# Weight and chunk stores issued from GpSimd's queue instead of SyncE's, in a fused Fourier-mixing and gated MLP kernel

## The chip, the cores and the metric

The kernel runs on one core of a Trainium2 chip. The metric is the device time of one execution in microseconds (us); the figure quoted for a kernel is the median of its runs. Engines are named as in the profile: PE is TensorE's matmuls and PEld its weight loads, DVE is VectorE, ACT is ScalarE, POOL is GpSimd and SP is SyncE. A DMA is issued by SP, ACT or POOL, each of which has a queue of its own; the bytes are moved by 16 DMA engines.

## The reference

`x` has 2048 rows of 512. It is normalised, passes through a Fourier mixing in one branch and an MLP in the other, and the two are multiplied and added to `x`:

```python
def _A_ref(x, dft_seq_re, dft_seq_im, dft_hid_re, dft_hid_im):
    a = jnp.einsum("bsd,ed->bse", x, dft_hid_re)
    b = jnp.einsum("bsd,ed->bse", x, dft_hid_im)
    return jnp.einsum("ts,bse->bte", dft_seq_re, a) - jnp.einsum("ts,bse->bte", dft_seq_im, b)

def _B_ref(x, w1, b1, w2, b2):
    h = jnp.einsum("bsd,df->bsf", x, w1) + b1
    r = jnp.where(h > 0, h, 0)
    return jnp.einsum("bsf,fd->bsd", r * r, w2) + b2

xn = _layernorm(x)
s = _A_ref(xn, A_dft_seq_re, A_dft_seq_im, A_dft_hid_re, A_dft_hid_im)
g = _silu(_B_ref(xn, B_w1, B_b1, B_w2, B_b2))
return x + s * g
```

The sequence matrices are 2048 x 2048, the hidden ones 512 x 512, `w1` is 512 x 1792 and `w2` 1792 x 512, all in float32.

## The kernel before, in words

Every float32 operand is split into a high part (ScalarE, `split_hi`, L134) and a low part (VectorE, `split_lo`, L137), and a product is made in three passes of matmuls. Most products are tiled two by two in Winograd's form: seven products instead of eight, with sums of the operands made by VectorE beforehand.

The kernel runs in this order. First the sequence matrices are multiplied with the normalised `x`, in 8 chunks of 256 rows (`c`), each in 8 steps (`j`). Chunks 0 and 1 are made in plain products (`products`, L368, matmuls at L377); chunks 2 to 7 in Winograd's form (the loop at L596, matmuls at L362). One step of chunks 2 to 7 takes 42 matmuls. Then come the products of the chunk results with the hidden matrices (`YUnit`), then those with `w1` (`HUnit`), then those with `w2` (from L1043), with the gate and the output.

A step's piece of the sequence matrix is 512 KB. SP loads it (`load_c`, L273) into one of three buffers tagged `u`. VectorE makes its sums in place (`step_sums`, L284 to L286), and ScalarE and VectorE split it into one of two buffers `ga` and `gb` (`step_split`, L320), from which TensorE reads. In step n the code makes the sums for step n + 2, splits for step n + 1, and issues the load for step n + 4. A load waits until the split has read the buffer's old contents.

Beside the steps, other work is made ahead. `EARLY` (L39) says at which step a piece of it is done:

- Weights: `weight` (L396) loads one weight's raw tiles on SP, makes its sums, splits them into a buffer `wd0` or `wd1`, and stores the result to device memory in two parts of 768 and 1024 KB (L412). This is done for the four hidden-matrix tiles (`d0` to `d3`, stored in `WDD`) and for three tiles of `w1` (`v0`, `v1`, `v6`, stored in `W1D`). They are read back much later: `WDD` by `load_wd` (L459, tiles named `wdp`), `W1D` by `load_w1` (L680).
- Chunk results: the eight results of a chunk are combined by VectorE during the next chunk's steps (`closing_of`, L335, operations at L343) into a buffer tagged `e`, 1024 KB. For chunks 2 to 6 it is stored to `PQD` when step 4 of the next chunk has made its last operation (L617). The results of chunks 0 and 1 (L562, L607) and of chunk 7 (L922) are stored elsewhere in the code. They are read back by `load_pq` (L419), from chunk 0's on.

The order on each engine is the order in which the code is written; there is no scheduler. A DMA-issuing engine takes its DMAs one after the other: a DMA that waits for its source or its buffer holds up those behind it on the same engine. SP issues all loads and, in this kernel, all stores but two kinds: the `w1` results and the mixing results, which ScalarE issues in its own queue (`hd<-h` and `y<-y`). POOL issues seven DMAs near the end, which add parts of `x` to the output tile in place (`add_x`, L899).

Of the kernel before, what the change touches and what calls it, by code (L numbers as in the profile page):

```python
# [8 lines left out]
F32 = mybir.dt.float32  # L9
# [119 lines left out]
def fnet_gated_kernel(ctx, tc, x, xt, ct, wd, w1, w2, b1, b2, out):  # L129
    nc = tc.nc  # L130
# [8 lines left out]
    def split(*parts):  # L139
        split_hi(*parts)  # L140
        split_lo(*parts)

    def copy(to, src, scale=1.0):
        nc.scalar.activation(to, src, AF.Copy, scale=scale)
# [12 lines left out]
    PQD = [dram.tile([P, 2, 4, 256], F32, name=f"pqd{c}") for c in range(NC)]  # L157
# [6 lines left out]
    def bank(tag, name):  # L164

        return acc.tile([P, 512], F32, tag=tag, name=name)

    def buf(tag, shape, name, dtype=F32):
        return pool.tile(shape, dtype, tag=tag, bufs=3 if tag == "u" else 1, name=name)
# [105 lines left out]
    def plain_parts(c, j, hs=slice(0, 2)):  # L275
        if (c, j) not in part:
            part[c, j] = operand_buf("g" + "ab"[j % 2], f"g{c}_{j}", 0 if (c, j) == (PLAIN - 1, NJ - 1) else 3 if j in TURNED else 1, (2, 4, CW))
        g, r = part[c, j], raw[c, j]
        s = slice(2 * hs.start, 2 * hs.stop)
        return g[:, HI, s], g[:, LO, s], r[:, s]  # L280
# [24 lines left out]
    def step_load(n):  # L305
        if n < len(steps):
            load_c(*steps[n])
        elif n - len(steps) + YFIRST < 6:
            y_load(n - len(steps) + YFIRST)

    def step_sums(n):
        if n < len(steps):
            u = raw[steps[n]]
            sums_b(u[:, 4:8], u)

    def step_split(n):
        if n < len(steps):
            s = steps[n]
            u = raw.pop(s)
            g = part[s] = buf("g" + "ab"[s[1] % 2], [P, 2, 7, CW], f"g{s[0]}_{s[1]}", F32R)  # L320
            split(g[:, HI], g[:, LO], u[:, 1:8])
# [13 lines left out]
    def closing_of(part_, ms, room):  # L335

        copy(part_(C21), halves(ms[1]))
        for k in room:
            copy(room[k], ms[k])
        for to, m, frm, op in ((C11, 2, C21, ALU.add), (C22, 6, C21, ALU.add), (C21, 7, C22, ALU.subtract),  # L340
                               (C12, 5, C22, ALU.subtract), (C22, 5, C21, ALU.add), (C12, 3, C12, ALU.add),
                               (C21, 4, C21, ALU.subtract)):
            nc.vector.tensor_tensor(part_(to), halves(room.get(m, ms[m])), part_(frm), op=op)  # L343
            yield
# [3 lines left out]
    def chunk_part(e):  # L348

        v = e.rearrange("p (h i m n) -> p h m i n", h=2, i=2, m=2)  # L350
        return lambda k: v[:, PART[k][0], PART[k][1]]

    def some(steps_, n):
        for _ in range(n):
            next(steps_)

    def mm(ps, w, mv, first, last):

        ps = ps.rearrange("p (i d t) -> p d i t", i=2, d=2)
        for d in range(2):  # L360
            for a_, b_ in PASSES:
                nc.tensor.matmul(ps[:, d], w[:, a_, d * P:(d + 1) * P], halves(mv(b_)),  # L362
                                 start=first and d == 0 and (a_, b_) == (HI, HI),
                                 stop=last and (a_, b_) == (LO, HI), skip_group_check=True)
# [21 lines left out]
    def go(*names):  # L386


        for v in names:
            if v[0] == "h" and int(v[1:]) >= NTC * NP:  # L390
                continue
            if v not in making:
                making[v] = makers[v[0]](int(v[1:]))
            next(making[v])

    def weight(n, raw_, sums_, to, k, e=None, turn=False):  # L396

        if e:
            e = buf(e, [P, 8, 256], f"{n}rt")
            r, t = e[:, 0:4], e[:, 4:8]  # L400
        else:
            r, t = buf("pq00", [P, 4, 256], f"{n}r"), buf("pq01", [P, 4, 256], f"{n}t")
        nc.sync.dma_start(r, raw_)
        yield
        if turn:
            copy(r[:, I22:I21 + 1], r[:, I22:I21 + 1], -1.0)
        sums_(t, r)
        yield
        g = buf(f"wd{int(k)}", [P, 2, 7, 256], f"{n}g", F32R)
        for q, src in ((slice(0, 3), r[:, 1:4]), (slice(3, 7), t)):  # L410
            split(g[:, HI, q], g[:, LO, q], src)
            nc.sync.dma_start(to[:, :, q], g[:, :, q].bitcast(F32))  # L412
            yield

    makers["d"] = lambda n: weight(f"wd{n}", wd[n], sums_b, WDD[n], n % 2, "e" if n == 1 else None, True)
    makers["v"] = lambda n: weight(f"w1{n}", w1[n], sums_w1, W1D[n], 0)

    def load_pq(n, x_):
# [84 lines left out]
    g = plain_parts(0, 1)  # L503
# [11 lines left out]
    for j in range(1, NJ):  # L515
# [19 lines left out]
        g = plain_parts(*order[j + 1])  # L535
# [51 lines left out]
    def last_out(k, op):  # L587
        to = last.rearrange("p (h i m d t) -> p h d m i t", h=2, i=2, m=2, d=2)[:, k // 2, k % 2]
        op(to, accs[1][k].rearrange("p (m i t) -> p m i t", m=2, i=2))
# [6 lines left out]
    for n, s in enumerate(steps):  # L596
        c, j = s
        if j == 0:
            ms = {k: bank(tag, f"m{k}_{c}") for k, tag in
                  {1: "bb", 2: "b20", 6: "b21", 3: "b30", 5: "b31", 7: "b32", 4: ("ba", "bc")[c % 2]}.items()}  # L600
        g = part.pop(s)
        for p in FIRST if j == 0 and c > PLAIN else ORDER:
            if p == 4 and n == 0:
                step_sums(2)
                step_split(1)
                last_out(3, copy)
                nc.sync.dma_start(PQD[1].rearrange("p h k n -> p (h k n)"), last)  # L607
            a, b = PRODUCTS[p]
            mm(ms[p], XC[j][:, a], lambda b_: g[:, b_, b], j == 0, j == NJ - 1)
        if n:  # L610
            step_sums(n + 2)
            step_split(n + 1)
        step_load(n + 4)
        if closing:
            some(closing, LATER.get(j, 0))
            if j == max(LATER):
                nc.sync.dma_start(PQD[c - 1].rearrange("p h k n -> p (h k n)"), e)  # L617
                closing = None
        if j == NJ - 1:
            e = buf("e", [P, 2048], f"c{c}")  # L620
            room = {}
            if c < NC - 1:
                room = buf("pq10", [P, 2, 512], f"left{c}")
                room = {7: room[:, 0], 5: room[:, 1], 3: buf("pq11", [P, 512], f"left3_{c}")}
            closing = closing_of(chunk_part(e), ms, room)
            some(closing, 2)
        if s == (PLAIN, 4):
            nc.vector.transpose(stats_t, stats.rearrange("p m h j -> p (m h j)"))
            for q in range(4):
                nc.sync.dma_start(rows[:, q * 32:(q + 1) * 32], stats_t[q * 32:(q + 1) * 32, :])  # L630
        go(*EARLY.get(s, ()))
# [326 lines left out]
    for u in range(2, NC):  # L958
        n = 2 * u + 2
# [83 lines left out]
    for n in range(NTC * NP):  # L1043
        c, p = divmod(n, NP)
# [37 lines left out]
        if p == NP - 1 and not last:  # L1082
            e = buf("e", [P, 4, 512], f"z{c}")
# [16 lines left out]
    e = buf("u", [P, 4, 512], f"z{c}")  # L1100
# [54 lines left out]
def _launch(arrays, out_shape):  # L1155
    import numpy as np
    import concourse.bacc as bacc
    from concourse.bass_utils import run_bass_kernel_spmd

    nc = bacc.Bacc("TRN2", target_bir_lowering=False, num_devices=1, dynamic_dma_scratch_size=1024)  # L1160
    feed, args = {}, []
    for name, v in arrays.items():
        v = np.ascontiguousarray(v)
        feed[f"in_{name}"] = v
        args.append(nc.dram_tensor(f"in_{name}", v.shape, mybir.dt.from_np(v.dtype), kind="ExternalInput").ap())
    args.append(nc.dram_tensor("out_0", out_shape, F32, kind="ExternalOutput").ap())
    with tile.TileContext(nc, schedule_with_timeline_sim=True) as tc:
        fnet_gated_kernel(tc, *args)
    r = run_bass_kernel_spmd(nc, [feed], core_ids=[0])
    return r.results[0]["out_0"]  # L1170
# [25 lines left out]
```

## Time and profile before

| | |
|---|---|
| time, median of 3 runs | 673.54 us (673.42 to 674.33) |
| time of the profiled execution | 673.52 us |
| its span, first to last instruction | 671.7 us |
| TensorE (PE) busy | 665.4 us, 99% of the span |
| VectorE (DVE) busy | 597.3 us, 89% |
| ScalarE (ACT) busy | 379.0 us, 56% |
| GpSimd (POOL) busy | 8.8 us, 1% |
| moved by DMA | 150.82 MB, mean 225 GB/s |

The profile is of one execution. Times are counted from the span's start. A row of a group or of a timeline gives the engine, the line of the code, the operation, what is written and read (`out<-in`), the count, and times in us; "idle before" is how long the engine had waited, and the arrow names what ended that wait. `SPq` stands for SP's queue of DMA-issuing instructions. "To landing" is the time from a DMA's issue to the completion that others can wait for.

### The profile page before, as it was taken

What the parts mean: (1) busy time and instruction counts of PE and PEld (TensorE: products, weight loads), DVE (VectorE), ACT (ScalarE), POOL (GpSimd) and SP (SyncE); (2) the same over time, 40 slices, a digit from 0 to 9 for tenths busy, and PEclk for the clock granted to TensorE, in tenths of its full rate; (3) what the DMA queues carried; (4) which work ended last, traced back from release to release, by engine and by line L of the source; (5) the groups of instructions that cost most, each with busy time, mean ns of one, the idle gap of its engine ahead of it and who ended that gap; (6) DMA issues with size and microseconds to landing.
All of it is one profiled execution on the core that took longest, in us unless ns stands there. A gap on an engine that the chain in (4) does not pass through costs nothing.

```text
span 671.7 us, 13186 instructions
## 1 busy us (share of the span) xinstructions
PE 665.4 (99%) x5438; PEld 646.5 (96%) x5438; DVE 597.3 (89%) x833; ACT 379.0 (56%) x524; POOL 8.8 (1%) x11
## 2 busy tenths in 40 slices
PE   8999999999999999999999999999999999999997
PEld 5888889999999999999999999999999999999997
DVE  7997888999999999799899989877887889999997
ACT  6856554534445454444365547788778765454451
POOL 0000000000000000000000000000000000101011
PEclk9999999999999999999999999999999999999999
DMA  8635768646556774759688557665755866777765
GB/s 306 212 100 218 255 232 277 214 148 213 211 168 225 248 286 162 261 164 344 200 296 279 194 188 297 222 246 209 267 183 198 326 241 212 181 230 176 232 205 156
DMA packets 51739, 150.82 MB, mean 225 GB/s; under 512 B 4960, under 2 KB 19552, under 8 KB 50272
## 3 DMA queue, kind: packets, MB, share of 16 engines
q1 hardware_dynamic: 43568, 129.28, 57.1%
q10 hardware_dynamic: 6208, 18.88, 7.1%
q0 software_dynamic: 1904, 1.84, 1.9%
q8 instruction: 42, 0.69, 0.4%
q14 instruction: 17, 0.14, 0.1%
HBM read 101.98 MB, written 47.99 MB: 223 GB/s over the span
## 4 chain that ended last, share of the span: by engine, by line
PE 94%; DVE 2%; DMA 2%; ACT 1%; issue 0%; SPq 0%; DVEq 0%; ACTq 0%
PE m L362 32%; PE m_o L861 15%; PE r_B L755 13%; PE r_A L755 9%; PE pq_b L377 8%; PE r_C L755 4%; PE r_D L755 4%; PE m_last L861 4%; PE pq_ba L377 2%; PE pq_bc L377 1%; PE pq_bb L377 1%; DMA u<-in_ct 1%; DMA x<-in_x 1%; DVE g L137 1%; DVE z L1111 0%; DVE z L911 0%
## 5 line engine op out<-in xcount | busy, mean ns | idle before, releaser
L362 PEld LDWEIGHTS m<-g,xc 128*128 128x128 f32 x2016 | 229.1, 188 | 0.3 <-DVE g L137 0.2
L362 PE MATMUL m<-g,xc 128*128 128x256 f32 x2016 | 229.3, 276 | 0.1
L134 ACT ACTIVATE g<-u 128x1792 fp32r<-128x1792 f32 (+2 forms) x65 | 99.0, 1523 | 132.1 <-PE m L362 92.6
L137 DVE TENSOR_TENSOR g<-u,g 128x1792 fp32r<-128x1792 f32 (+2 forms) x65 | 116.8, 1797 | 19.3 <-ACT g L134 18.8
L861 PE MATMUL m_o<-w,g 128*128 128x256 f32 x882 | 100.5, 276 | 0.0
L861 PEld LDWEIGHTS m_o<-w,g 128*128 128x128 f32 x882 | 100.3, 188 | 0.0
L134 ACT ACTIVATE g<-hr 128x1792 fp32r<-128x1792 f32 (+2 forms) x31 | 48.2, 1566 | 39.9 <-DVE hr L296 17.7
L755 PE MATMUL r_B<-xT,w 128*128 128x256 f32 x504 | 66.5, 276 | 0.0
L377 PE MATMUL pq_b<-g,xc 128*128 128x512 f32 x240 | 65.2, 391 | 1.0 <-ACT xc L134 1.0
L755 PEld LDWEIGHTS r_B<-xT,w 128*128 128x128 f32 x504 | 61.4, 188 | 0.0
L137 DVE TENSOR_TENSOR g<-hr,g 128x1792 fp32r<-128x1792 f32 (+2 forms) x31 | 56.7, 1838 | 3.0 <-ACT g L134 2.8
L377 PEld LDWEIGHTS pq_b<-g,xc 128*128 128x128 f32 x240 | 44.8, 188 | 11.3 <-ACT xc L134 1.9
L755 PE MATMUL r_A<-xT,w 128*128 128x256 f32 x336 | 42.8, 276 | 0.0
L755 PEld LDWEIGHTS r_A<-xT,w 128*128 128x128 f32 x336 | 40.2, 188 | 0.0
L755 PE MATMUL r_B<-wdp,yg 128*128 128x256 f32 x288 | 35.9, 277 | 0.0
L284 DVE TENSOR_TENSOR u<-u 128x512 f32<-128x512 f32 x48 | 32.9, 685 | 3.0 <-DMA u<-in_ct 3.0
L755 PEld LDWEIGHTS r_B<-wdp,yg 128*128 128x128 f32 x288 | 34.1, 188 | 0.1
L861 PE MATMUL m_last<-w,g 128*128 128x256 f32 x294 | 33.5, 276 | 0.0
L861 PEld LDWEIGHTS m_last<-w,g 128*128 128x128 f32 x294 | 33.4, 188 | 0.0
L137 DVE TENSOR_TENSOR yg<-yraw,yg 128x1792 fp32r<-128x1792 f32 x13 | 26.2, 2018 | 0.7 <-ACT yg L134 0.7
L134 ACT ACTIVATE yg<-yraw 128x1792 fp32r<-128x1792 f32 x13 | 22.2, 1707 | 5.4 <-DVE yraw L293 4.4
L755 PE MATMUL r_D<-xT,w 128*128 128x256 f32 x168 | 23.6, 276 | 0.0
(187 smaller groups left out, 876.8 us busy)
## 6 DMA issues: line engine op xcount, KB each, us to landing
u<-in_ct SPq DMA_DIRECT2D x63, 512.0 KB, 3.9
hd<-h ACTq DMA_DIRECT2D x28, 512.0 KB, 4.0
hr<-hd SPq DMA_DIRECT2D x28, 512.0 KB, 3.7
wdp<-wdd SPq DMA_DIRECT2D x8, 896.0 KB, 7.2
yraw<-pqd SPq DMA_DIRECT2D x13, 512.0 KB, 6.0
pqd<-c SPq DMA_DIRECT2D x6, 1024.0 KB, 6.2
w<-w1d SPq DMA_DIRECT2D x6, 896.0 KB, 8.2
y<-y ACTq DMA_DIRECT2D x8, 512.0 KB, 5.5
```

Source lines behind the costliest of these rows:

```text
L134: nc.scalar.activation(hi, src, AF.Copy)
L137: nc.vector.tensor_tensor(lo, src, hi.bitcast(F32), op=ALU.subtract)
L284: nc.vector.tensor_tensor(t[:, 0:2], r[:, 0:1].to_broadcast([P, 2, 256]), r[:, 1:3], op=ALU.add)
L362: nc.tensor.matmul(ps[:, d], w[:, a_, d * P:(d + 1) * P], halves(mv(b_)), start=first and d == 0 and (a_, b_) == (HI, HI), stop=last and ( ...
L377: nc.tensor.matmul(accs[c][k], w, part[c, j][:, b_, 2 * h:2 * h + 2], start=j == 0 and h == 0 and (a_, b_) == (HI, HI), stop=j == NJ - 1 a ...
L755: nc.tensor.matmul(self.region(REGION[k]), w, mv, start=i == 0 and k in (1, 7), stop=i == len(ops) - 1, skip_group_check=True)
L861: nc.tensor.matmul(m[:, i * 256:(i + 1) * 256], ready[n][:, a_, H_SLOT[a], i * P:(i + 1) * P], W2[p][:, b_, b], start=p == 0 and i == 0 an ...
```

## The change

The store of each part of a weight (L412) and the store of a chunk's result in the loop over the steps (L617) are issued by POOL in place of SP. The loads, the other stores and all arithmetic stay where they are.

```diff
@@ -409,7 +409,7 @@
         g = buf(f"wd{int(k)}", [P, 2, 7, 256], f"{n}g", F32R)
         for q, src in ((slice(0, 3), r[:, 1:4]), (slice(3, 7), t)):
             split(g[:, HI, q], g[:, LO, q], src)
-            nc.sync.dma_start(to[:, :, q], g[:, :, q].bitcast(F32))
+            nc.gpsimd.dma_start(to[:, :, q], g[:, :, q].bitcast(F32))
             yield
 
@@ -614,7 +614,7 @@
         if closing:
             some(closing, LATER.get(j, 0))
             if j == max(LATER):
-                nc.sync.dma_start(PQD[c - 1].rearrange("p h k n -> p (h k n)"), e)
+                nc.gpsimd.dma_start(PQD[c - 1].rearrange("p h k n -> p (h k n)"), e)
                 closing = None
```

On SP's queue, at step 4 of chunk 6, the change reads as follows (`-` is gone; `u7_0` and `u7_1` are pieces of the sequence matrix loaded ahead for chunk 7, `wdp0` a stored weight that is loaded back in two halves, `pqd5` the stored result of chunk 5):

```order
 L459 DMA wdp0_2852<-wdd0_83 128x1792
 L273 DMA u7_0_2902<-in_ct 128x1024
-L617 DMA pqd5_80<-c5_2626 128x2048
 L459 DMA wdp0_2852<-wdd0_83 128x1792
 L273 DMA u7_1_2955<-in_ct 128x1024
```

The store is gone from between the two loads, and the second half of `wdp0` follows `u7_0` directly.

On POOL's queue, the later stores and the first of the adds near the end (`w1d1` and `w1d6` are tiles of `w1`, `z0` the output tile; `+` is new):

```order
+L412 DMA w1d1_88<-w11g_2081 256x1x768
+L412 DMA w1d1_88<-w11g_2081 256x1x1024
+L617 DMA pqd4_79<-c4_2188 128x2048
+L412 DMA w1d6_89<-w16g_2519 256x1x768
+L412 DMA w1d6_89<-w16g_2519 256x1x1024
+L617 DMA pqd5_80<-c5_2626 128x2048
+L617 DMA pqd6_81<-c6_3057 128x2048
 L899 DMA z0_6599<-in_x 128x2x256 x2
```

POOL had nothing to issue before that first add; now 19 stores stand ahead of it.

## The prediction

> **What bounds the kernel now.** I read the busy time by stretches first, then what TensorE waited for, then the one place where the chain of waits leaves TensorE, and last the queues. Busy time by stretches (start:end, length, then busy us and instruction count of PE, PEld, DVE, ACT and POOL, granted clock, DMA share, GB/s):
>
> ```profile
> 0.00:20.00 20.00, 17.77 (x68) 12.52 (x69) 16.42 (x43) 13.96 (x31) 0.20 (x4) 1.00 0.80 289
> 20.00:635.00 615.00, 614.95 (x5085) 601.51 (x5084) 549.23 (x746) 351.77 (x479) 5.00 (x4) 1.00 0.66 225
> 635.00:671.70 36.70, 32.70 (x289) 32.50 (x287) 31.64 (x46) 13.27 (x16) 3.65 (x3) 0.98 0.64 185
> ...
> 95.00:270.00 175.00, 175.00 (x1546) 174.95 (x1545) 161.63 (x203) 81.84 (x66) 0.00 (x0) 1.00 0.63 217
> 270.00:325.00 55.00, 54.95 (x482) 54.75 (x481) 47.76 (x59) 25.03 (x21) 0.00 (x0) 1.00 0.74 258
> ```
>
> TensorE is busy 614.95 of the 615 us from 20 to 635, at a granted clock of 1.00. It is idle for 2.23 us of the start and 4.00 us of the end, and the change touches neither. All moved stores are issued between 73 and 311 us. So whatever they cost or free there is worth something only as far as it makes TensorE wait, or stops it from waiting. It waits there at one place that the trace shows; the weight loads, SP's queue and VectorE around it (start, us, engine, line, what; in brackets the idle time before it and what ended it):
>
> ```profile
> 285.82 1.84 PEld L362 LDWEIGHTS m<-g,xc 128*128 128x128 f32 x15 [0.25 <-DVE g L137]
> ...
> 270.72 0.33 SPq L273 DMA_DIRECT2D u<-in_ct  x1
> 271.32 0.33 SPq L617 DMA_DIRECT2D pqd<-c  x1
> 271.70 0.42 SPq L459 DMA_DIRECT2D wdp<-wdd  x1
> 275.26 0.33 SPq L273 DMA_DIRECT2D u<-in_ct  x1
> ...
> 277.97 2.03 DVE L137 TENSOR_TENSOR g<-u,g 128x1792 fp32r<-128x1792 f32 x1 [1.22 <-ACT g L134]
> 282.22 0.69 DVE L284 TENSOR_TENSOR u<-u 128x512 f32<-128x512 f32 x1 [2.23 <-DMA u<-in_ct]
> 282.95 0.43 DVE L285 TENSOR_TENSOR u<-u 128x256 f32<-128x256 f32 x1
> 283.41 0.43 DVE L286 TENSOR_TENSOR u<-u 128x256 f32<-128x256 f32 x1
> 283.75 2.02 DVE L137 TENSOR_TENSOR g<-u,g 128x1792 fp32r<-128x1792 f32 x1
> ```
>
> The load of u issued at 275.26 stands in SP's queue behind a chunk store (271.32) and half a weight load (271.70). VectorE idles 2.23 us for it, makes its sums, and then the split at 283.75 whose end (285.77) TensorE waits for: 0.25 us. How long u loads take from issue to landing, first that one alone, then all 36 issued between 95 and 270:
>
> ```profile
> DMA to landing us min/median/max: 6.9/6.9/6.9
> ...
> DMA to landing us min/median/max: 3.4/3.9/6.0
> ```
>
> This gives the yardstick for the rest: a u load that lands 6.9 us after its issue costs TensorE 0.25 us, so one that lands within about 6.9 - 0.25 = 6.7 us costs nothing. All 36 others are inside it.
>
> **The change part by part.** Seven weights are stored in two parts each and five chunks in one: 14 + 5 = 19 stores leave SP's queue.
>
> What SP gets back. The rows of three of the 19 stores (issue times in ns, min/median/max), and SP's waits (us, times, longest):
>
> ```profile
> L412 SPq DMA_DIRECT2D w1d<-w10g x2: 524/524/525, 161.9 to 166.9; - x2
> L617 SPq DMA_DIRECT2D pqd<-c x5: 320/326/327, 157.1 to 310.0; - x5
> ...
> SPq L273 <- DVE g L137: 200.8, 54, 5.6
> SPq L412 <- DVE wd0g L137: 3.5, 2, 2.4
> SPq L617 <- DVE c L343: 1.2, 5, 0.3
> ```
>
> 14 x 0.52 + 5 x 0.33 = 8.9 us of issuing and a few us of waiting at the stores. It is hidden already: the u loads behind the stores wait 200.8 us for VectorE's split to give their buffer free, so SP reaches them early with the stores or without them. Worth 0 us; without that cover a load would start at most one issue, 0.52 us, sooner.
>
> What POOL takes on. Its only DMAs now, with POOL's idle time and VectorE's work beside the first one, and the usual length of two of those VectorE operations:
>
> ```profile
> L899 POOL DMA_DIRECT2D z<-in_x x7 | 8.7, 1236 | 652.9 <-DVE z L911 607.1 <-DMA fin<-y 29.3 <-DMA fin<-in_x 7.6
> ...
> 575.46 1.33 POOL L899 DMA_DIRECT2D z<-in_x  x1 [575.01 <-DVE z L911]
> 575.66 0.68 DVE L290 TENSOR_TENSOR hr<-hr 128x512 f32<-128x512 f32 x1
> 576.38 0.42 DVE L295 TENSOR_TENSOR hr<-hr 128x256 f32<-128x256 f32 x1
> ...
> L290 DVE TENSOR_TENSOR hr<-hr 128x512 f32<-128x512 f32 x28 | 19.2, 685 | 0.0
> L295 DVE TENSOR_TENSOR hr<-hr 128x256 f32<-128x256 f32 x25 | 10.6, 425 | 0.9
> ```
>
> Issuing one costs POOL 1.24 us, so 19 cost 23.5 us on an engine that has nothing to do until 575. Nothing of POOL's own is queued behind them but these seven adds, over 260 us after the last store. VectorE's operations beside the issue last 0.68 and 0.42 us, as everywhere (685 and 425 ns). Worth 0 us.
>
> When the stores land. POOL begins them up to 1.24 - 0.33 = 0.9 us later than SP did. Nobody reads them soon; what matters is when their source buffer is written again. The tightest is the chunk buffer:
>
> ```profile
> 157.08 0.33 SPq L617 DMA_DIRECT2D pqd<-c  x1
> ...
> 168.36 0.58 ACT L144 ACTIVATE c<-m 128x512 f32<-128x512 f32 x1
> ...
> pqd<-c SPq DMA_DIRECT2D x6, 1024.0 KB, 6.2
> z<-in_x POOLq DMA_DIRECT2D x7, 256.0 KB, 4.9
> hd<-h ACTq DMA_DIRECT2D x28, 512.0 KB, 4.0
> ```
>
> The store is issued at 157.08 and lands after 6.2 us; ScalarE writes the next chunk there at 168.36. The cover is 11.3 - 6.2 = 5.1 us. Worth 0 us; if the store took 5.1 us more, ScalarE and then the PSUM banks would be late.
>
> What the loads gain or lose. A u load no longer stands behind a store, but its bytes share the 16 DMA engines with it. Packets' time per queue, as a share of 16 engines' span:
>
> ```profile
> q1 hardware_dynamic: 43568, 129.28, 57.1%
> q10 hardware_dynamic: 6208, 18.88, 7.1%
> q0 software_dynamic: 1904, 1.84, 1.9%
> ```
>
> Times 671.7 us, a MB takes 2.97 us on SP's queue (q1), 2.53 on ScalarE's (q10) and 6.94 on POOL's (q0). q10 carries stores only, from a queue of their own beside SP's loads; q0's seven transfers add to their target, and so move each byte more than once. A moved store is a plain copy like q10's, so I take its rate: no extra time, and the load at 275.26 lands between 6.9 us (bytes in the same order) and some 3 us sooner (the 1 MB store behind it): a gain of 0 to 0.25 us. The other bound is q0's rate: 1.05 MB x (6.94 - 2.97) = 4.2 us more in each chunk store.
>
> The order of work on TensorE, VectorE and ScalarE is unchanged, and on POOL the stores stand in the order in which VectorE finishes their sources, so none holds up another that is ready.
>
> The sum: the profiled execution took 673.52 us (671.7 of span and 1.8 around it); 0 for SP, 0 for POOL, 0 for the landing, 0 to -0.25 for the load at 275.26. That is 673.3 to 673.5, and I say 673.4; the median of the three runs, 673.54, is the profiled execution's within 0.02.
>
> **The rivals.** *Software packets are slow, and loads run late.* If q0's 6.94 us per MB is the queue's and not the addition's, then each chunk store takes 4.2 us more of the engines. A load beside it would share that time with it, half and half: 2.1 us. At 275.26 TensorE pays the 2.1 us. Beside the three chunk stores ahead of it a load of at most 6.0 us becomes 8.1, and TensorE pays 8.1 - 6.7 = 1.4 each time: 2.1 + 4.2 = 6.3 us, 679.8 us; if the whole 4.2 us fell on the load each time, 4.2 + 3 x 3.5 = 14.7 us, 688.2. It decides from about 1.35 us of lateness in all. For it: the trace has no plain copy on q0. Against it: an addition reads its target too. The Trainium skill has a rule here, in "DMA: Bandwidth & Descriptors", section "Queues, rings and completion order": each DMA engine takes turns between the queues at packet granularity. By that rule a load loses half the engines to a store that it was ahead of in SP's queue; no row here shows the turns, and with plain packets the same bytes end at the same time, which leaves 673.4.
>
> *GpSimd holds VectorE up.* If every issue blocked VectorE for its 1.24 us: 13 of the 19 fall between 95 and 270 us, 16.1 us, where VectorE has 175.00 - 161.63 = 13.4 us left. 2.7 us would reach TensorE: 676.2 us. Against it stand the unchanged 0.68 and 0.42 us beside POOL's issue at 575.46. The Trainium skill ("SBUF — State Buffer", section "Who interferes with whom") says that an operation of VectorE with two inputs in SBUF contends with a GpSimd instruction that reads SBUF, not with one that only writes; by that rule a descriptor write holds up nothing, and the trace agrees with its 0.68 us.
>
> *The stores keep their buffers too long.* Over the 5.1 us of cover, ScalarE's first write to the next chunk waits. At the 4.2 us of the first rival and 0.9 us of later issue the sum is just 5.1: it begins there and nowhere below it, and would add to 679.8.
>
> *Clearly faster.* Over 0.2% (1.35 us, about the least that a measurement of this kernel tells from no change) is more than TensorE's whole idle time from 20 to 635, 0.05 us by the stretches and 0.25 by the wait. Only a cause that the profile doesn't show could give it: say 671.9.
>
> **How the numbers follow.** The forecast, 673.4, has 0.75; its own range is 672.8 to 674.2 (the gain of 0.25 and 0.3 to 0.6 us between runs). Slow packets with or without held buffers get 0.13 (679.8), GpSimd holding VectorE up 0.08 (676.2), clearly faster 0.04 (671.9). Slower by over 0.2% is 0.13 + 0.08 = 0.21, faster 0.04, within it 0.75. The range that is to hold 8 in 10 takes the forecast's and the mild beginnings of the two slower cases: 672.7 to 675.6.
>
> **What would show it.** Right: TensorE still busy for 615 of 615 us from 20 to 635; the wait near 285 the same 0.25 us or gone; u loads from 95 to 270 landing by 6.0 us at most; POOL busy about 32 us instead of 8.8; VectorE's splits still 2.02 us; q0 at some 20 MB with about 2.5 to 3 us per MB. Wrong: u loads over 6.7 us with "DVE u <- DMA u<-in_ct" among VectorE's waits and PEld waiting for g at several places (slow packets); splits over 2.02 us under POOL's issues (VectorE held up); ScalarE waiting for a store before it writes c (buffers). The prediction falls if TensorE's idle time between 73 and 325 us moves by over 1.35 us for any cause.

## The result, and the profile after

The changed kernel takes 674.75 us (median of 12 runs, 673.93 to 676.16), the kernel before 673.29 us (median of 12, 672.65 to 674.33). The ratio is 1.0023 with a 95% interval of 1.0015 to 1.0031: 1.0 to 2.1 us slower. Measured again it was 1.0024 (1.0015 to 1.0033). So the change costs about 1.5 us, just over the 0.2% that was set as the limit of "no change" (the intervals reach below it), and on the side that had 0.21 of the chances.

The profiled execution of the changed kernel took 674.05 us, one of the short ones, with a span of 672.3 us. Its queues (packets, MB, share of 16 engines' span) and the stretches shown before:

```profile
q1 hardware_dynamic: 39040, 111.19, 50.3%
q0 software_dynamic: 5536, 19.92, 8.6%
q10 hardware_dynamic: 6208, 18.88, 7.1%
```

```profile
20.00:635.00 615.00, 614.87 (x5086) 601.39 (x5085) 549.42 (x746) 352.10 (x480) 17.39 (x23) 1.00 0.66 225
635.00:672.30 37.30, 32.70 (x289) 32.50 (x287) 31.65 (x46) 13.28 (x16) 3.62 (x3) 0.97 0.65 181
...
95.00:270.00 175.00, 175.00 (x1545) 174.91 (x1544) 161.78 (x204) 82.10 (x66) 8.50 (x13) 1.00 0.62 217
270.00:325.00 55.00, 54.87 (x484) 54.67 (x483) 47.90 (x59) 25.06 (x21) 1.08 (x2) 1.00 0.75 262
```

The stores did move: q0 went from 1.84 to 19.92 MB. TensorE is still full from 95 to 270 us, and VectorE's 161.78 us there are the 161.63 of before. What differs is small and stands at two places: 270 to 325 us, and the end, where the stretch from 635 us on grew from 36.70 to 37.30 us with TensorE's 32.70 us unchanged.

**The place near 275 us.** Timelines of the changed kernel, of SP, POOL, VectorE and the weight loads, and the landing of the load of u issued at 275.50:

```profile
270.97 0.33 SPq L273 DMA_DIRECT2D u<-in_ct  x1
271.35 0.42 SPq L459 DMA_DIRECT2D wdp<-wdd  x1
275.50 0.33 SPq L273 DMA_DIRECT2D u<-in_ct  x1
...
271.95 0.55 POOL L617 DMA_DIRECT2D pqd<-c  x1 [27.56 <-DVE c L343]
...
282.56 0.69 DVE L284 TENSOR_TENSOR u<-u 128x512 f32<-128x512 f32 x1 [2.32 <-DMA u<-in_ct]
...
286.16 1.93 PEld L362 LDWEIGHTS m<-g,xc 128*128 128x128 f32 x16 [0.33 <-DVE g L137]
...
DMA to landing us min/median/max: 7.0/7.0/7.0
```

The chunk store is POOL's now and no longer ahead of the load of u at 275.50. That load still lands late, after 7.0 us (6.9 before): VectorE idles 2.32 us for it (2.23 before), and TensorE waits 0.33 us (0.25 before). The DMA engines in four stretches around it (start:end, length, busy us of PE, PEld, DVE, ACT, POOL, clock, DMA share, GB/s), before:

```profile
273.00:275.00 2.00, 2.00 (x20) 2.00 (x19) 1.79 (x1) 0.17 (x1) 0.00 (x0) 1.00 0.94 377
275.00:277.00 2.00, 2.00 (x20) 2.00 (x19) 1.68 (x4) 0.77 (x1) 0.00 (x0) 1.00 1.02 415
277.00:279.00 2.00, 2.00 (x20) 2.00 (x19) 1.03 (x1) 0.94 (x1) 0.00 (x0) 1.00 0.99 409
279.00:281.00 2.00, 2.00 (x20) 2.00 (x20) 0.99 (x1) 0.01 (x1) 0.00 (x0) 1.00 0.54 210
```

and in the changed kernel:

```profile
273.00:275.00 2.00, 2.00 (x20) 2.00 (x20) 1.61 (x2) 0.42 (x1) 0.00 (x0) 1.00 1.07 359
275.00:277.00 2.00, 2.00 (x20) 2.00 (x19) 1.93 (x4) 0.53 (x1) 0.00 (x0) 1.00 0.95 238
277.00:279.00 2.00, 2.00 (x20) 2.00 (x19) 0.79 (x1) 1.18 (x1) 0.00 (x0) 1.00 1.01 427
279.00:281.00 2.00, 2.00 (x20) 2.00 (x20) 1.24 (x1) 0.00 (x0) 0.00 (x0) 1.00 0.93 373
```

The last two columns are the finding. From 275 to 277 us the engines are as busy as before (0.95) and move 238 GB/s in place of 415: 2 us x 177 GB/s = 0.35 MB less, which takes 0.85 us at 415 GB/s, and is made up from 279 to 281. By the packet records, nearly all bytes of this slow stretch are the weight load's (SP, 271.35): the store's first packet comes only at 276.96, 5.0 us after its issue, when 114 of the weight load's 128 packets of 7 KB have begun. Those 114 took 411 ns on average. In the kernel before, the same load's packets took 272 ns.

**The end.** After VectorE's last operation come the last waits and a few closing steps. SP's and POOL's of these, before and after (count, ns, first and last start):

```profile
L1167 SPq EVENT_SEMAPHORE  x10: 17/28/28, 669.5 to 671.7; - x10
L1167 SPq DRAIN  x3: 7/7/7, 670.9 to 671.2; - x3
L1167 POOLq DRAIN  x2: 34/64/94, 671.2 to 671.5; - x2
L1167 POOLq EVENT_SEMAPHORE  x4: 17/17/17, 671.0 to 671.6; - x4
```

```profile
L1167 SPq EVENT_SEMAPHORE  x11: 17/28/28, 669.5 to 672.2; - x11
L1167 SPq DRAIN  x3: 7/7/7, 671.1 to 671.4; - x3
L1167 POOLq DRAIN  x2: 46/70/94, 671.4 to 671.6; - x2
L1167 POOLq EVENT_SEMAPHORE  x4: 17/17/17, 671.2 to 672.2; - x4
```

VectorE's last operation starts at 668.62 and 668.63 us, so the two executions are level there. SP is through its waits 0.2 us later (first drain 671.1 against 670.9), and POOL pauses between its last drain and its last semaphores: 0.1 us before, 0.4 us now in the trace (671.65 to 672.09). Together the way from VectorE's last operation to the end is 3.10 us before and 3.65 after.

### The profile page after: what moved, and what is told of

Read it like the earlier page. It is cut to its first block, busy times and chain, and to the rows that moved or that the text cites. A ratio compares the mean times of both kernels' runs of the same rounds, so it can differ in the third digit from the quotient of the medians.

```text
span 672.3 us, 13206 instructions
## 1 busy us (share of the span) xinstructions
PE 664.9 (99%) x5438; PEld 645.8 (96%) x5438; DVE 597.3 (89%) x833; ACT 379.0 (56%) x524; POOL 21.2 (3%) x30
## 3 DMA queue, kind: packets, MB, share of 16 engines
q0 software_dynamic: 5536, 19.92, 8.6%
## 4 chain that ended last, share of the span: by engine, by line
PE 95%; DVE 2%; DMA 2%; ACT 1%; issue 0%; SPq 0%; DVEq 0%; ACTq 0%
PE m L362 32%; PE m_o L861 15%; PE r_B L755 13%; PE r_A L755 9%; PE pq_b L377 8%; PE r_C L755 4%; PE r_D L755 4%; PE m_last L861 4%; DMA u<-in_ct 2%; PE pq_ba L377 2%; PE pq_bb L377 2%; PE pq_bc L377 2%; DVE g L137 1%; DVE z L1111 0%; DVE z L911 0%; ACT g L134 0%
```

## The experiments

Theory A: one load of u, near 275 us, lands late because of the chunk store beside it. Theory B: the end of the program is longer with GpSimd's stores, wherever they are. Each was measured beside the kernel before. The number that opens each answer is the ratio of its time to that of the kernel before, with the 95% interval; 0.001 is 0.67 us. The profiles give three numbers for each, collected in a table at the end of this section.

**The change again.**

> The changed kernel once more, for a second profile beside its times. Theory A (a load of u lands late): over half of the 1.5 us stands in waits of TensorE between 73 and 325 us, at the loads of u that run beside a store, and the second profile shows them larger than the first, which lost 0.08 us there. Theory B (the end of the program): the main part is as before, and 0.5 to 0.7 us stand behind VectorE's last operation, in SP's last waits and in GpSimd's last steps. Time by both: 1.0 to 2.0 us over the kernel before.

1.0024 (1.0015 to 1.0033). Its profiled execution (674.15 us) was again a short one: TensorE waits 0.57 us near 286, and the end takes 3.66 us:

```profile
286.22 1.93 PEld L362 LDWEIGHTS m<-g,xc 128*128 128x128 f32 x16 [0.57 <-DVE g L137]
```

Both places show up, the end unchanged, the load larger. TensorE's whole loss at the load is 0.69 us (see the table), somewhat under the half of 1.5 us that theory A expected.

**Weight stores alone.** Only the first of the two edits:

```diff
-            nc.sync.dma_start(to[:, :, q], g[:, :, q].bitcast(F32))
+            nc.gpsimd.dma_start(to[:, :, q], g[:, :, q].bitcast(F32))
```

> Only the 14 stores of weights are GpSimd's, the five of chunk results are SP's again. Theory A: the chunk store stands ahead of the load of u near 275 us as before, so the time is within 0.4 us of before. Theory B: 14 GpSimd stores make the program and the last waits as long as 19 do, nearly, so 0.8 to 1.5 us slower than before.

1.0011 (1.0003 to 1.0020), 0.2 to 1.3 us. The load of u lands after 6.5 us and TensorE does not wait there; the end takes 3.47 us. B has its share here, 0.37 us by the profile: SP is through its waits that much later, and POOL's pause of 0.4 us is absent. A's limit of 0.4 us is passed by the median and not by the interval.

**Chunk stores alone.** Only the second edit.

> Only the five stores of chunk results are GpSimd's. Theory A: 1.0 to 1.5 us slower than before, as the whole change. Theory B: between before and the change, 0.2 to 0.6 us slower, since GpSimd's program grows by 5 DMAs and not by 19.

1.0023 (1.0014 to 1.0032), as much as the whole change. The load of u lands after 7.7 us, and TensorE waits 1.04 us:

```profile
286.93 1.25 PEld L362 LDWEIGHTS m<-g,xc 128*128 128x128 f32 x10 [1.04 <-DVE g L137]
```

Five of the 19 stores cost as much as all 19, which B alone cannot explain. The two halves, 0.7 and 1.5 us, add to more than the whole; their intervals (0.2 to 1.3 and 0.9 to 2.2) leave room for that, and no run shows more.

**Small stores beside.** The kernel before, with a small GpSimd store next to each of the 19:

```diff
             nc.sync.dma_start(to[:, :, q], g[:, :, q].bitcast(F32))
+            nc.gpsimd.dma_start(tiny[next(tag)], g[0:16, 0, q.start].bitcast(F32))
...
                 nc.sync.dma_start(PQD[c - 1].rearrange("p h k n -> p (h k n)"), e)
+                nc.gpsimd.dma_start(tiny[next(tag)], e[0:16, 0:256])
```

> The kernel before, with all 19 stores on SP, and beside each of them a GpSimd store of 16 rows of 1 KB of the same tile into memory that nobody reads. Theory A: 16 KB delay no load, so the time is as before, within 0.3 us. Theory B: the 19 issues, their semaphores and their instructions are all there, so it is 1.0 to 1.5 us slower, as the change.

1.0009 (1.0000 to 1.0018). The end takes 3.47 us, with POOL's pause of 0.4 us in it, while SP, which has the extra semaphore here too, is through its waits as early as before; the load of u is on time (6.6 us). Neither theory's number: by the profile B is real, at about half of what it was taken for; the time alone, 0.0 to 1.2 us longer, barely tells it from nothing. TensorE also waits 0.20 us at 109.42 us, outside the table's stretch, where a load of u issued at 99.07 took 6.7 us.

**The kernel before again.**

> The kernel before once more, for a second profile of it. The load of u issued near 275 us took 6.5 to 6.9 us in the three profiles that have the chunk store on SP, and 7.0 to 7.7 us in the three that have it on GpSimd. If that is the stores' queue: 6.4 to 6.9 us again, TensorE losing 0 to 0.7 us there, and 3.1 us from VectorE's last operation to the end. If it is chance from run to run: anywhere between 6.5 and 7.7.

1.0001 (0.9992 to 1.0010). The load lands after 6.4 us, TensorE loses nothing there, 3.09 us at the end. Near 275 us the rate is that of the first profile:

```profile
275.00:277.00 2.00, 2.00 (x20) 2.00 (x20) 1.93 (x4) 0.45 (x1) 0.00 (x0) 1.00 1.00 392
```

So the 0.25 us wait in the first profile of before, which the prediction's gain hung on, is in one of its two profiles, and in one of the five that have this chunk store on SP and the weight load where it was.

**One chunk store back on SP**, that of chunk 5, near 271 us:

```diff
-                nc.gpsimd.dma_start(PQD[c - 1].rearrange("p h k n -> p (h k n)"), e)
+                (nc.sync if c - 1 == 5 else nc.gpsimd).dma_start(PQD[c - 1].rearrange("p h k n -> p (h k n)"), e)
```

> The change, but for the one chunk store near 271 us, which SP issues again. If that store alone makes the load of u late: the load lands within 6.9 us, and the time falls from 1.4 us over before to 0.4 to 0.8, which is the longer end. If the other chunk stores or the weight stores cost as well: it stays over 1.1 us.

1.0006 (0.9997 to 1.0014). Near 275 us it reads like the kernel before:

```profile
275.00:277.00 2.00, 2.00 (x21) 2.00 (x19) 1.55 (x4) 1.00 (x1) 0.00 (x0) 1.00 1.01 395
```

395 GB/s, and the load lands after 6.5 us. One store of 19 put back removes most of the cost: the interval ends below that of the change. (POOL's pause was gone too, with 18 GpSimd stores in place of 19, and the end took 3.23 us: part of the saving is that.)

**The weight load earlier.** In `EARLY` the load of `wdp0` (its two halves, SP at 266.12 and 271.70 us) moves one step ahead; on SP (first) and with the change (second):

```diff
-    (6, 1): ("y1",), (6, 3): ("y1", "p0"), (6, 4): ("p0",),
+    (6, 1): ("y1",), (6, 2): ("p0",), (6, 3): ("y1", "p0"),
```

> The kernel before, all stores on SP, with the two halves of the weight load that runs at 266 and 272 us made one step (4.8 us) earlier, so that the load of u at 275 us has the chunk store ahead of it, but no longer the weight load behind that. If lateness there costs TensorE its 0 to 0.7 us: the load lands within 6.0 us, no wait near 285, 0.2 to 0.7 us faster than before. If not: as before.

1.0000 (0.9992 to 1.0009). The load of u lands after 4.6 us, as expected, and no time is won: there was hardly a wait to remove, as the second profile of before says.

> The change, with the weight load made one step earlier in the same way. If the change's cost is that load of u and the end of the program: only the end is left, 0.4 to 0.8 us slower than before, with no wait near 285. If GpSimd's stores cost elsewhere: over 1.1 us.

1.0013 (1.0004 to 1.0022). The load lands after 5.2 us, TensorE does not wait near 285, and the end takes 3.66 us. By the profile, with the weight load out of the way, the change keeps the cost of its end and loses the rest. The time, 0.9 us (0.3 to 1.5), lies under the 1.1 us of the other case and above the 0.4 to 0.8 expected, and its interval overlaps that of the change, so it supports this reading without proving it.

**Chunk stores on ScalarE's queue**, weight stores on SP:

```diff
-                nc.sync.dma_start(PQD[c - 1].rearrange("p h k n -> p (h k n)"), e)
+                nc.scalar.dma_start(PQD[c - 1].rearrange("p h k n -> p (h k n)"), e)
```

> The kernel before with the five chunk stores issued by ScalarE, whose queue is a hardware one like SP's, and the weight stores on SP. If a second queue of any kind makes the engines slower beside the weight load: the load of u near 275 us lands after 7.0 to 7.7 us, with some 240 GB/s between 275 and 277 us in place of 390 to 415, and 0.5 to 1.0 us slower than before. If it is GpSimd's software queue: 6.4 to 6.9 us, 390 to 415 GB/s, as before within 0.3 us.

1.0007 (0.9998 to 1.0016). ScalarE issued the store at 271.18 us. The slow stretch is there, 2 us sooner than with GpSimd:

```profile
273.00:275.00 2.00, 2.00 (x20) 2.00 (x19) 1.63 (x1) 0.34 (x1) 0.00 (x0) 1.00 0.99 249
275.00:277.00 2.00, 2.00 (x20) 2.00 (x20) 1.85 (x4) 0.92 (x1) 0.00 (x0) 1.00 1.00 392
```

249 GB/s at a share of 0.99, the load landing after 7.0 us, TensorE losing 0.71 us. So it is not the software queue as such: at this place a store in any second queue beside the weight load is enough. By time alone this kernel is not told from before.

**Eight more GpSimd instructions**, added to the change with the weight load earlier:

```diff
+    for _ in range(8):
+        nc.gpsimd.memset(stats_t[:, 0:1], 0.0)
```

> The change with the weight load one step earlier (so that the load of u is on time), and eight more GpSimd instructions at the start, each a memset of one column that is overwritten later. If GpSimd's 0.4 us pause between its last two steps is the fetching of instructions at a place that its program's length sets: the pause falls from 0.44 to about 0.08 us, from VectorE's last operation to the end 3.2 to 3.5 us in place of 3.66, and 0.2 to 0.6 us slower than before. If the pause comes from the stores themselves: 0.44 again.

1.0002 (0.9992 to 1.0012). POOL's last steps:

```profile
L1169 POOLq DRAIN  x2: 46/68/89, 671.9 to 672.2; - x2
L1169 POOLq EVENT_SEMAPHORE  x4: 17/17/17, 671.8 to 672.4; - x4
```

The pause is gone (0.1 us between the last drain and what follows) and the end takes 3.30 us, with all 19 stores in place. So the pause is not the stores' own doing: it changes with the length of GpSimd's program. That it is the fetching of instructions is an inference. The time does not settle the expected 0.2 to 0.6 us: the ratio allows 0.5 us faster to 0.8 slower, and the medians, 674.0 and 673.37 us, lie 0.6 apart.

**One chunk store alone on GpSimd**, that of chunk 5, the reverse of the one put back:

> The kernel before with one store of the 19 moved to GpSimd: that of the chunk near 271 us. If that store makes the load of u late: it lands after 7.0 to 7.7 us, 225 to 240 GB/s between 275 and 277 us, and with 0.1 to 0.3 us for the longer end 0.6 to 1.3 us slower than before. If the stores cost together: under 0.4 us.

1.0013 (1.0004 to 1.0022): 0.3 to 1.5 us for a single moved store.

```profile
275.00:277.00 2.00, 2.00 (x20) 2.00 (x20) 1.67 (x4) 0.78 (x1) 0.00 (x0) 1.00 0.92 239
```

239 GB/s, landing after 7.2 us, and only 3.16 us at the end.

**All profiles together.** Landing is that of the load of u issued near 275 us; "TensorE late" is by how much the matmuls from 270 to 325 us take longer than at 113.3 ns each, their rate when nothing waits; "end" is from the start of VectorE's last operation to the end of the span.

| kernel | store of chunk 5 on | landing us | TensorE late us | end us | ratio |
|---|---|---|---|---|---|
| before | SP | 6.9 | 0.70 | 3.10 | |
| before again | SP | 6.4 | 0.00 | 3.09 | 1.0001 |
| weight stores alone | SP | 6.5 | 0.00 | 3.47 | 1.0011 |
| small stores beside | SP | 6.6 | 0.00 | 3.47 | 1.0009 |
| one chunk store on SP | SP | 6.5 | 0.00 | 3.23 | 1.0006 |
| the change | POOL | 7.0 | 0.45 | 3.65 | 1.0023 |
| the change again | POOL | 7.3 | 0.69 | 3.66 | 1.0024 |
| chunk stores alone | POOL | 7.7 | 1.50 | 3.41 | 1.0023 |
| one chunk store alone | POOL | 7.2 | 0.65 | 3.16 | 1.0013 |
| chunk stores on ScalarE | ACT | 7.0 | 0.71 | 3.09 | 1.0007 |
| weight load earlier | SP | 4.6 | 0.13 | 3.10 | 1.0000 |
| the change, weight load earlier | POOL | 5.2 | 0.00 | 3.66 | 1.0013 |
| the same, longer GpSimd program | POOL | 3.5 | 0.54 (a later load of u, 7.0) | 3.30 | 1.0002 |

With the weight load where it was, the landing is 6.4 to 6.9 us in five profiles with the store on SP, 7.0 to 7.7 in four with it on POOL; the nearest two are only 0.1 us apart. The weight load's packets part the two groups clearly: they took 272 to 274 ns on average in the five, 396 to 467 in the four, and 370 with the store on ScalarE.

TensorE's mean loss there is 0.14 us in the five and 0.82 in the four: 0.7 us. The longer end is 3.65 - 3.10 = 0.55 us. The sum is 1.25 us, inside the measured 1.0 to 2.1.

This sum pools kernels that differ in their other stores. By the two profiles of the change and the two of before alone, the loss at the load differs by only 0.57 - 0.35 = 0.22 us, and the sum is 0.8 us. Both profiled executions of the change were among its shortest, and the loss varies between executions. The loss as counted also holds something that is not waiting: in the first profile of before and in that of the chunk stores alone, some 75 matmuls after the wait run at 118 ns in place of 113, at a recorded clock of 1.00, which makes about 0.35 us in each and stays unexplained. What is left of the measured time is within the spread between runs and was not placed; the start alone shifts the whole program by up to 0.9 us from profile to profile, whatever the kernel.

## Why the prediction was wrong, by its own steps

The time lay inside the range (672.7 to 675.6), the direction did not come true: 673.4 with "no change" was forecast, and it became slower by a little over 0.2%. That the range held the time is luck as far as the causes go: it reached up to 675.6 for slow packets and a held-up VectorE, and neither occurred.

*Where to look* was half right. TensorE stays full outside the start, the end and the one place near 285 us, and that place did change. But of the idle time at the start and the end the prediction said that "the change touches neither", and the end grew by 0.55 us. Its sign of being wrong looked only at TensorE between 73 and 325 us; there the busy time fell by 0.1 and 0.3 us in the two profiles, far from the 1.35 us that it named. The yardstick of 6.7 us held roughly: loads of u that landed by 6.6 us cost nothing there, those that took 6.9 us or more cost 0.45 to 1.5. The cost of 0.25 us that it put on a landing of 6.9 counts the idle time alone; the matmuls around that wait started 0.36 us late.

*The load at 275.26* is the step that failed. The sum gave it "0 to -0.25" us, on the ground of "bytes in the same order" and, among the rivals, that "with plain packets the same bytes end at the same time". They don't: with the store in a queue of its own, the engines moved 225 to 239 GB/s for 2 us (four profiles) in place of 387 to 415 (five), because the weight load's packets took longer, and the load of u came 0.7 us later in the mean, not earlier. The place had been named, and so had the lack of slack (a load at 6.9 us has none left), but the working kept the engines' rate constant under the new order. Its gain was also read from one profile, whose 0.25 us wait the second profile of before did not have.

*"Worth 0 us" for GpSimd* failed at the end of the program, which the working left out: it asked only what GpSimd has to do until 575 us. SP has one more semaphore to wait for (x11 in place of x10 above) and is done 0.2 us later, and POOL, with its longer program, pauses 0.4 us in its closing steps in place of 0.1: 0.55 us together.

*The moved stores' rate* was right. From the two pages' q0 rows, (8.6 - 1.9)% of about 672 us for 19.92 - 1.84 = 18.08 MB is 2.5 us per MB, that of ScalarE's queue (2.53) which the working took; so the rival of slow software packets falls, though it pointed at the right load. GpSimd's issue was taken too dear: 0.55 us for a chunk store (the row above), not 1.24, so POOL was busy 21.2 us and not the 32 expected; nothing waited for it.

*GpSimd holding VectorE up* did not happen: VectorE's 161.78 us from 95 to 270, with 13 issues beside them, stand against 161.63. The trace agrees with the Trainium skill ("SBUF — State Buffer", section "Who interferes with whom") as cited in the prediction.

*The Trainium skill's rule of turns* ("DMA: Bandwidth & Descriptors", section "Queues, rings and completion order") bears on the place, but it is about who goes next and not about the bytes moved in a busy us; that these fall from 415 to 238 GB/s is not in it. In the changed kernel's packet records no turns are seen until the weight load has 14 of its 128 packets left; with the store on ScalarE's queue, the two queues move about equal shares from 276 to 278 us.

*Buffers kept too long* was not seen: the change's profile has no wait of ScalarE or VectorE for a store between 60 and 325 us.

Still open is why the weight load's packets are slower there. They are slow while the store has been issued in the other queue and none of its own packets is recorded yet (411 ns in place of 272). It is not that the weight load now stands directly behind a load of u: moved one step earlier it also does, with no store waiting, and its packets took 279 ns on SP and 282 with the change. Nor does every such meeting do it: near 310 us a chunk store on POOL again meets weight loads, and in the 3 us after its issue their packets took 275 to 282 ns in all six profiles that have it there (273 before). Whether the store's reads, its writes or the order of the two queues makes the difference was not tried.

## What to carry to other kernels

When TensorE is full and one load stands at the edge of its slack, a store taken out of that load's queue can make it later rather than earlier: here another load, no longer behind the store, was moved at little more than half the rate for 2 us. Look at GB/s beside the DMA share in the few us around the load, and place the transfers apart before choosing queues. A queue that was idle is not free either: here it added 0.55 us of waits and closing steps at the program's end. And where an expected gain is a quarter of a us in one profile, take a second profile before counting it.

## What the runs showed of the hardware that was not expected

A busy share of the DMA engines says little about bytes here: 0.95 went with 238 GB/s and 1.02 with 415, at the same place of two kernels. GpSimd's plain store packets are as quick as SP's: 314 ns for 8 KB on q0 in the changed kernel, 319 on SP's queue before. And the closing steps of this program vary with the length of GpSimd's instruction stream: a pause of 0.4 us came with 19 stores and went with 18, and with 19 and eight instructions more.
